# K and v steps chunk by chunk over three banks, with matmuls that keep the stationary operand

## The chip, the cores and the metric

One core of one Trainium2 chip. The metric is the device time of one execution in microseconds; the median of three runs stands for the kernel. TensorE multiplies (its weight loads are listed as an engine of their own, PEld), VectorE (DVE), ScalarE (ACT) and GpSimd (POOL) do the elementwise work, SyncE (SP) issues nearly all DMAs.

## The reference

x has 2048 tokens of 640 features. Branch A is a linear attention with 32 heads of 20 features, branch B a gated feed-forward block with 1728 hidden features; a sigmoid gate for each token mixes them.

```python
qkv = x @ wqkv                               # q, k, v: 32 heads of 20
pq, pk = q @ w_phi[h], k @ w_phi[h]          # head by head
phi_q = concat(softmax(pq), softmax(-pq))    # 40 features for each head
phi_k = concat(softmax(pk), softmax(-pk))
kv, z = phi_k^T v, sum_s phi_k
a = ((phi_q kv) / (phi_q z + 1e-6)) @ wo
b = (silu(x @ w_gate) * (x @ w_up)) @ w_down
out = g * a + (1 - g) * b                    # g = sigmoid(sum(x * gate_w))
```

## The kernel before

**Work.** Tokens go in 16 tiles of 128 (t), four of which make a group of 512 (bt). w_phi is multiplied into the k and q weights on the chip first, so that one product of x with wkv gives pk, a few columns of pq, v and the argument of the gate. There are four kinds of work on TensorE:

- gate and up for 14 blocks of hidden features (k) of a group: five matmuls of 512 columns each, then tanh and a copy on ScalarE, one operation on VectorE and one on GpSimd, which leave a block of hT
- a **k step** for each token tile (`ktile`, `features` with which = 1): 1441 columns of wkv in three parts, of 460 (the end of pk, q columns and some v), 481 (most of v and the gate) and 500 columns (the start of pk), each the sum over five chunks c of 128 input features. The stationary operand is the tile of x, `xT[:, c, tok]`; the weights are streamed
- a **q step** for each tile (480 columns of wq), whose features are turned by a DMA transpose, multiplied by the summed kv (`num`), divided, turned again and multiplied by wo (`wo`, and `worest` for the last 128 output features of a group)
- the sums over hT (`down` for each tile, `rest` for the last 128 output features of a group, `edge` for the last 64 hidden features)

**A k step before.** `features` adds three tasks, first (460 columns), main (481) and m_ (500), the second and third ordered behind the one before. Each goes through all five chunks into one bank of PSUM. The parts of 500 and 460 columns lie in a pair of neighbouring banks ("pair", key ps), the 481 in a third bank (key v). All three banks are taken when the first task starts. `vtail` evacuates: lines 991 and 993 copy the v part of the 460 columns (they count as writing the bank, so the max on VectorE waits for them), then line 996 copies the 480 columns of v and line 998 takes the tanh of the gate's column, which releases the bank "v". VectorE takes max (line 1066) and min (1070) and subtracts (1074, 1078), which releases the pair; then follow exp on ScalarE, sum (1089) and reciprocal (1093) on VectorE, the norm on GpSimd (1099) and a DMA transpose that SP issues (line 1115).

**Order.** `_Plan` works out the order of everything beforehand: each task has an engine, a cost, what it depends on, buffers that it takes and releases, a priority and for some a time before which it isn't begun ("hold", `K_AT + K_EACH * t` for k steps, `Q_AT + Q_EACH * t` for q steps). At every moment each engine gets its most urgent task that is ready and for whose buffers there is room; the program is written out in that order, and semaphore waits are put where the data needs them. So each engine runs a fixed order. `SUMS` gives the order of a group's sums around its edge ("x"), `D_AFTER` after which block of the next group they come. There are 8 banks of PSUM for all of it.

**A list of matmuls.** `mms` takes a list of (output, stationary, moving, first, last), works out the waits once for the whole list and issues one `pe.matmul` for each entry; each is a weight load and a matmul. The last one signals the semaphore.

Of the kernel before, what the change touches and what calls it, by code (L numbers as in the profile page):

```python
# [6 lines left out]
P = 128  # L7
# [15 lines left out]
VC = VG * GH * DH  # L23
# [6 lines left out]
VLO = VX + D - VC - DH  # L30
KVW = VLO + VC + 2
KB = 500
KOFF = 512 - KB
# [218 lines left out]
class _Plan:  # L252
# [11 lines left out]
    def add(self, eng, cost, fn, deps=(), prio=5.0, lat=None, acq=(), rel=(), name=""):  # L264
        t = _Task(eng, cost, fn, deps, prio, self.LAT[eng] if lat is None else lat,
                  tuple(acq), tuple(rel), len(self.tasks), name)
        self.tasks.append(t)
        return t
# [84 lines left out]
def _mm(*cols):  # L353
    return sum(c / 2400.0 + 0.003 for c in cols)


def _build(
# [13 lines left out]
    pe, act, dve, pool, sp = nc.tensor, nc.scalar, nc.vector, nc.gpsimd, nc.sync  # L371
# [8 lines left out]
    def sb(name, shape, dtype):  # L380
        t = nc.alloc_sbuf_tensor(name, list(shape), dtype)
        tr.reg_tensor(t, "sbuf", nc.lookup_mloc(t).addr, rowelems(shape), mybir.dt.size(dtype))
        return t
# [6 lines left out]
    xT = sb("xT", [P, 5, S_TOK], BF16)  # L390
    wq = sb("wq", [P, 5, QW], BF16)
    wkv = sb("wkv", [P, 5, KVW], BF16)
# [40 lines left out]
    ps = nc.alloc_psum_tensor("ps", [P, 8 * 512], F32)  # L433
# [6 lines left out]
    add = plan.add  # L440

    def bank(i, j, c0, c1, r0=0, r1=P):
        return ps[r0:r1, (2 * i + j) * 512 + c0:(2 * i + j) * 512 + c1]

    def one(b, c0, c1, r0=0, r1=P):
        return ps[r0:r1, b * 512 + c0:b * 512 + c1]

    def wide(i, n=D):
        return ps[:, 2 * i * 512:2 * i * 512 + n]

    def mms(groups):

        reads = [g[1] for g in groups] + [g[2] for g in groups]
        writes = []
        seen = set()
        for g in groups:
            k = (g[0].offset, str(g[0].ap))
            if k not in seen:
                seen.add(k)
                writes.append(g[0])  # L460

        def fn():
            last = None
            for o, l, r, st, sp_ in groups:
                last = pe.matmul(o, lhsT=l, rhs=r, start=st, stop=sp_, skip_group_check=True)  # L465
            return last
        return run("pe", fn, reads=reads, writes=writes)

# [82 lines left out]
    gw_l = add("act", 0.5, load_gate, prio=-7, lat=6.0, name="gw")  # L551
# [11 lines left out]
    def load_head(key, c0, c1, k0, k1, land, prio):  # L563
        w, src = (wg, gsrc) if key == "g" else (wu, usrc)
        t = load("sp", w[:, c0:c1, k0 * P:k1 * P], src[:, c0:c1, k0 * P:k1 * P], land, prio)
        for k in range(k0, k1):
# [17 lines left out]
    wv_l = [vx_l, load("sp", wkv[:, :, VX:VLO], rows(A_wqkv[:, 2 * D + VC:3 * D - DH]), 31.2, -35),  # L584
            load("sp", wkv[:, :, VLO:VLO + VC], rows(A_wqkv[:, 2 * D:2 * D + VC]), 32.0, -34.9)]
# [12 lines left out]
    xl = [x_[4] for x_ in xs]  # L598
# [153 lines left out]
        for k in range(HD):  # L752
            ffn_tail(0, k, cs[k], (last["g", k], last["u", k]), 0)

    K_AT, K_EACH, Q_AT, Q_EACH = 30.00, 6.722, 137.19, 6.955
    PRE_Q = 10.14
    PRE_EACH = 2.3
    PRE_AT = 23.6
    PRE_X = 27.0
    D_AFTER = 3  # L760
    FIN_DVE = 12
    SUMS = ((0, -1, "x", 1, 2, 3), (0, -1, "x", 1, 2, 3), (-1, 0, "x", 1, 2, 3), (0, -1, "x", 2, 1, 3))
    K_PAIRS = 9
    store_t = {}
    gs_t = {}
# [67 lines left out]
    def early(bt, j):  # L833
        return SUMS[bt].index(j) < SUMS[bt].index("x")

# [179 lines left out]
    def features(t, which, wq_l, prio, ctx):  # L1015

        tok = slice(t * P, (t + 1) * P)
        bt = t // 4  # L1020

        def cols(o_, w_, c0, c1):
            return lambda: mms(acc(o_(), [(xT[:, c, tok], w_[:, c, c0:c1]) for c in range(5)]))
        w_ = wkv if which else wq
        got = [("pair" if which else "bank", ctx, "ps"), ("phi", ctx, "phi"), ("st", ctx, "st"), ("pp", ctx, "pp")]
        ng = NKQ if which else NQ
        nh = GH * ng

        def cost(k, q):
            return k if which else q  # L1030
        if which:
            before = [kvp_t.get((bt - 2, h)) for h in range(2)]
            first = add("pe", _mm(*([VLO - KB] * 5)), cols(lambda: bank(ctx["ps"], 1, 0, VLO - KB), w_, KB, VLO),
                        deps=[xl[bt], gw_l] + wv_l + wq_l + before, prio=prio, acq=got + [("bank", ctx, "v")], name="p1")
            main = add("pe", _mm(*([VC + 1] * 5)), cols(lambda: one(ctx["v"], 0, VC + 1), w_, VLO, VLO + VC + 1), prio=0.0, name="v")
            main.after = first
            m_ = add("pe", _mm(*([KB] * 5)), cols(lambda: bank(ctx["ps"], 0, KOFF, 512), w_, 0, KB), prio=0.0, name="p1")
            m_.after = main
            vt = vtail(t, ctx, (first, main))
            start = first  # L1040
        else:
            start = m_ = add("pe", _mm(*([QW] * 5)), cols(lambda: one(ctx["ps"], 0, QW), w_, 0, QW), deps=[xl[bt]] + wq_l, prio=prio, acq=got, name="p0")
            vt = None
        start.hold = K_AT + K_EACH * t if which else Q_AT + Q_EACH * t

        def dst():
            return phi[:, ctx["phi"], 0:ng, 0:GF]

        def src():
            return wide(ctx["ps"], KOFF + nh * DH)[:, KOFF:KOFF + nh * DH] if which else one(ctx["ps"], 0, QW)  # L1050

        def pv():
            return src().rearrange("p (h f) -> p h f", f=DH)

        def pg():
            return src().rearrange("p (g k f) -> p g k f", k=GH, f=DH)

        def sv(sg):
            return dst().rearrange("p g (k s f) -> p g k s f", s=2, f=DH)[:, :, :, sg, :]

        def bc(tile):
            return tile[:, ctx["st"], 0:nh].rearrange("p (g k) -> p g k", k=GH).unsqueeze(3).to_broadcast([P, ng, GH, DH])

        def f_mx():
            a, b = mx[:, ctx["st"], 0:nh], pv()
            dveop(lambda: dve.tensor_reduce(a, b, AX.X, ALU.max), [b], [a])  # L1066

        def f_mn():
            a, b = mn[:, ctx["st"], 0:nh], pv()
            dveop(lambda: dve.tensor_reduce(a, b, AX.X, ALU.min), [b], [a])  # L1070

        def f_sp():
            o_, a, b = sv(0), pg(), bc(mx)
            dveop(lambda: dve.tensor_tensor(o_, a, b, ALU.subtract), [a, mx[:, ctx["st"], 0:nh]], [o_])  # L1074

        def f_sn():
            o_, a, b = sv(1), bc(mn), pg()
            dveop(lambda: dve.tensor_tensor(o_, a, b, ALU.subtract), [b, mn[:, ctx["st"], 0:nh]], [o_])  # L1078
        age = 2.5 + 0.01 * (t + (0 if which else NT))
        a1 = add("dve", cost(0.935, 0.565), f_mx, deps=[m_, vt], prio=age, name="max")  # L1080
        a2 = add("dve", cost(0.935, 0.565), f_mn, deps=[m_], prio=age, name="min")
        a3 = add("dve", cost(0.935, 0.565), f_sp, deps=[a1, a2], prio=age, name="sub")
        a4 = add("dve", cost(0.935, 0.565), f_sn, deps=[a2, a3], prio=age, rel=[got[0], ("pp", ctx, "pp")], name="sub")
        x1 = add("act", cost(1.5, 0.92), lambda: actop(dst(), dst(), ACTF.Exp), deps=[a4], prio=2, name="exp")

        def f_sm():
            a = sm[:, ctx["st"], 0:2 * nh].rearrange("p (g k) -> p g k", k=2 * GH)
            b = dst().rearrange("p g (k f) -> p g k f", f=DH)
            dveop(lambda: dve.tensor_reduce(a, b, AX.X, ALU.add), [b], [a])  # L1089

        def f_rc():
            a, b = rc[:, ctx["st"], 0:2 * nh], sm[:, ctx["st"], 0:2 * nh]
            dveop(lambda: dve.reciprocal(a, b), [b], [a])  # L1093

        def f_nm():
            a = dst().rearrange("p g (k f) -> p g k f", f=DH)
            r = rc[:, ctx["st"], 0:2 * nh]
            b = r.rearrange("p (g k) -> p g k", k=2 * GH).unsqueeze(3).to_broadcast([P, ng, 2 * GH, DH])
            poolop(lambda: pool.tensor_tensor(a, a, b, ALU.mult), [a, r], [a])  # L1099
        b1 = add("dve", cost(1.825, 1.075), f_sm, deps=[x1], prio=age, name="sum")  # L1100
        b2 = add("dve", cost(0.57, 0.37), f_rc, deps=[b1], prio=age, name="rec")
        return add("pool", cost(3.03, 1.75), f_nm, deps=[b2], prio=1, rel=[("st", ctx, "st")], name="norm")
# [140 lines left out]
    pre_k = premult_k(wkT_l, 2.0, PRE_AT)  # L1243
    pre_x = premult_x(wxT_l, 2.1, PRE_X)
    pre_q = premult_q(wqT_l, PRE_Q, 0.02)
# [7 lines left out]
    def downs_of(bt):  # L1253
        return [("d", j, bt) for j in SUMS[bt]]
    seq = [("f", k, bt) for k in range(K_PAIRS) for bt in range(2) if bt or k >= HD]
    seq += [("f", k, 0) for k in range(K_PAIRS, NK)]
    for bt in range(1, NBT):
        for k in range(K_PAIRS if bt == 1 else 0, NK):
            seq.append(("f", k, bt))
            if k == K_PAIRS * (bt == 1) + D_AFTER:  # L1260
                seq += downs_of(bt - 1)
# [72 lines left out]
```

## Time and profile before

| | us |
|---|---|
| median of 3 runs (285.13 to 285.67) | 285.41 |
| the profiled execution | 285.48 |
| its span | 283.7 |
| TensorE matmul busy / weight load busy | 278.8 / 137.2 |
| VectorE busy | 225.9 |
| ScalarE busy | 152.5 |
| GpSimd busy | 166.4 |
| matmuls of a k step, 3 x 80 records | 18.1 + 18.9 + 19.5 |
| granted TensorE clock | 1.00 |

The span is from the first to the last thing that the profiler saw. The time of the execution has some 1.8 us more around it. "PE" is the matmul, "PEld" the weight load, which runs beside it. Matmuls overlap one another, so their listed durations are longer than the distance from one start to the next. Most work of TensorE goes through one line of the program, 465, so shapes and names of tiles tell the groups apart: `ps<-wkv,xT` is a k step, `ps<-xT,wg` and `ps<-xT,wu` are gate and up, `ps<-v,phi` the products of features and v, `ps<-wd,hT` and `ps<-hT,wd` the sums over hT.

### The profile page before, as it was taken

The numbers are of one execution on the slowest core, as the hardware profiler recorded it, in microseconds if no ns is written. First come the engines' busy times: TensorE is split into PE (matmuls) and PEld (weight loads), VectorE is DVE, ScalarE is ACT, GpSimd is POOL, SyncE is SP. The second block draws the span as 40 slices with busy tenths as digits, with TensorE's granted clock in tenths as the row PEclk, the third lists the DMA queues.
The fourth block names the chain that finished last, engine by engine and source line by source line (L and its number), as shares of the span: only waits on it lengthen the run. The fifth ranks groups of instructions, "written<-read, shape, count | busy, mean of one in ns | idle before, by whom it ended". The sixth has DMA issues, their size and how long they took to land.

```text
span 283.7 us, 4489 instructions
## 1 busy us (share of the span) xinstructions
PE 278.8 (98%) x1671; PEld 137.2 (48%) x1700; DVE 225.9 (80%) x332; ACT 152.5 (54%) x272; POOL 166.4 (59%) x140
## 2 busy tenths in 40 slices
PE   8999999999999999999999999999999999999996
PEld 3444544444654455444544454454444454554543
DVE  0323369999899998999979989999989999974223
ACT  2555746777867465565634654566624666453320
POOL 4199613686667546447575394696865975962100
PEclk9999999999999999999999999999999999999999
DMA  7999999943000011000001021433556347254312
GB/s 169 270 126 147 288 228 160 288 145 72 14 16 2 12 25 37 14 2 14 17 14 32 15 52 38 83 62 60 62 116 177 58 84 190 59 103 85 116 37 92
DMA packets 74511, 25.41 MB, mean 90 GB/s; under 512 B 62585, under 2 KB 74489, under 8 KB 74489
## 3 DMA queue, kind: packets, MB, share of 16 engines
q1 hardware_dynamic: 73177, 25.10, 41.0%
q8 instruction: 13, 0.21, 0.3%
q10 hardware_dynamic: 1312, 0.03, 0.3%
q14 instruction: 9, 0.07, 0.1%
HBM read 8.46 MB, written 2.62 MB: 39 GB/s over the span
## 4 chain that ended last, share of the span: by engine, by line
PE 98%; issue 1%; DVE 0%
PE ps L465 97%; PE ps L645 2%; DVE xsb L795 0%
## 5 line engine op out<-in xcount | busy, mean ns | idle before, releaser
L695 POOL TENSOR_TENSOR hT<-hT,us 128x512 bf16<-128x512 bf16 (+1 forms) x56 | 62.2, 1119 | 56.9 <-DVE hT L686 30.0
L1099 POOL TENSOR_TENSOR phi<-phi,rc 128x1680 bf16<-128x1680 bf16 (+1 forms) x32 | 77.5, 2423 | 28.8 <-DVE rc L1093 28.6
L465 PE MATMUL ps<-xT,wg 128*128 128x512 bf16 (+1 forms) x287 | 67.2, 366 | 0.8
L465 PE MATMUL ps<-xT,wu 128*128 128x512 bf16 x254 | 63.1, 379 | 0.3
L686 DVE SCALAR_TENSOR_TENSOR hT<-hT,ps 128x512 bf16<-128x512 bf16 (+1 forms) x60 | 38.4, 644 | 29.5 <-ACT hT L475 26.9
L475 ACT ACTIVATE hT<-ps 128x512 bf16<-128x512 f32 (+1 forms) x60 | 33.8, 566 | 37.8 <-PE ps L465 37.5
L475 ACT ACTIVATE phi<-phi 128x1680 bf16<-128x1680 bf16 (+1 forms) x32 | 41.6, 1300 | 18.6 <-DVE phi L1078 18.5
L465 PE MATMUL ps<-wkv,xT 128*128 128x460 bf16 (+2 forms) x240 | 51.0, 366 | 0.1
L1089 DVE TENSOR_REDUCE sm<-phi 128x84 f32<-128x1680 bf16 (+1 forms) x32 | 48.3, 1512 | 3.0 <-ACT phi L475 3.0
L465 PE MATMUL ps<-wd,hT 128*128 128x512 bf16 (+4 forms) x230 | 48.6, 366 | 0.4
L465 PEld LDWEIGHTS ps<-xT,wg 128*128 128x128 bf16 x300 | 28.2, 98 | 29.3 <-issue 1.6
L690 ACT ACTIVATE us<-ps 128x512 bf16<-128x512 f32 (+1 forms) x60 | 33.7, 567 | 13.6 <-PE ps L465 12.3
L465 PEld LDWEIGHTS ps<-xT,wu 128*128 128x128 bf16 x260 | 25.4, 98 | 30.7 <-ACT xb L475 0.4
L465 PEld LDWEIGHTS ps<-wkv,xT 128*128 128x128 bf16 x240 | 23.2, 98 | 24.7
L465 PEld LDWEIGHTS ps<-wd,hT 128*128 128x128 bf16 (+1 forms) x238 | 21.7, 98 | 22.7 <-issue 0.2
L1066 DVE TENSOR_REDUCE mx<-ps 128x42 f32<-128x840 f32 (+1 forms) x32 | 26.4, 826 | 6.2 <-PE ps L465 6.2
L1070 DVE TENSOR_REDUCE mn<-ps 128x42 f32<-128x840 f32 (+1 forms) x32 | 26.6, 832 | 0.0
L1078 DVE TENSOR_TENSOR phi<-mn,ps 128x840 bf16<-128x840 f32 (+1 forms) x32 | 26.3, 821 | 0.3
L1074 DVE TENSOR_TENSOR phi<-ps,mx 128x840 bf16<-128x840 f32 (+1 forms) x32 | 26.4, 825 | 0.0
L807 POOL TENSOR_TENSOR xsb<-xsb,xb 128x512 bf16<-128x512 bf16 x12 | 13.8, 1151 | 13.4 <-ACT xb L475 13.4
L465 PE MATMUL ps<-wo,oT 128*128 128x512 bf16 x79 | 19.7, 379 | 0.1
L465 PE MATMUL ps<-wq,xT 128*128 128x480 bf16 x80 | 18.7, 366 | 0.0
(60 smaller groups left out, 206.6 us busy)
## 6 DMA issues: line engine op xcount, KB each, us to landing
out_dram<-xsb SPq DMA_DIRECT2D x15, 160.0 KB, 2.0
wd<-in_B_w_down_dram SPq DMA_DIRECT2D x1, 2080.0 KB, 9.7
wg<-in_B_w_gate_dram SPq DMA_DIRECT2D x2, 400.0 KB, 5.6
wu<-in_B_w_up_dram SPq DMA_DIRECT2D x2, 400.0 KB, 5.8
wo<-in_A_wo_dram SPq DMA_DIRECT2D x1, 800.0 KB, 5.5
wg<-in_B_w_gate_dram SPq DMA_DIRECT2D x2, 320.0 KB, 4.3
wu<-in_B_w_up_dram SPq DMA_DIRECT2D x2, 320.0 KB, 4.9
wkv<-in_A_wqkv_dram SPq DMA_DIRECT2D x1, 600.0 KB, 6.1
```

Of the source, the lines that this page charges most:

```text
L465: last = pe.matmul(o, lhsT=l, rhs=r, start=st, stop=sp_, skip_group_check=True)
L475: run("act", lambda: act.activation(o, i, func, scale=scale), reads=reads, writes=[o])
L686: dveop(lambda: dve.scalar_tensor_tensor(out=h, in0=h, scalar=1.0, in1=g_, op0=ALU.add, op1=ALU.mult), [h, g_], [h])
L690: run("act", lambda: act.activation(o_, u_, ACTF.Copy, scale=0.5), reads=[u_], writes=[o_] if k < 13 else [o_, u_])
L695: poolop(lambda: pool.tensor_tensor(h, h, u_, ALU.mult), [h, u_], [h])
L807: poolop(lambda: pool.tensor_tensor(x_, x_, b_, ALU.add), [x_, b_], [x_])
L1066: dveop(lambda: dve.tensor_reduce(a, b, AX.X, ALU.max), [b], [a])
L1070: dveop(lambda: dve.tensor_reduce(a, b, AX.X, ALU.min), [b], [a])
L1074: dveop(lambda: dve.tensor_tensor(o_, a, b, ALU.subtract), [a, mx[:, ctx["st"], 0:nh]], [o_])
L1078: dveop(lambda: dve.tensor_tensor(o_, a, b, ALU.subtract), [b, mn[:, ctx["st"], 0:nh]], [o_])
L1089: dveop(lambda: dve.tensor_reduce(a, b, AX.X, ALU.add), [b], [a])
L1099: poolop(lambda: pool.tensor_tensor(a, a, b, ALU.mult), [a, r], [a])
```

## The change

`mms` remembers the stationary operand of the entry before. Where an entry of the same list has the same one, it is issued by `again`, a matmul instruction that is marked to come without a weight load. Only the k steps have such entries one after another: their three tasks become one, and its list goes chunk by chunk, in each chunk the 460, the 481 and the 500 columns, so that the second and third matmul of a chunk find their operand in place. One task means one signal at the end: the copies of v, which waited for the first or the second task, now wait for the whole step. The plan's cost of the step is the sum of the three. Further, the due times of k and q steps, the earliest time of one weight product (PRE_X), D_AFTER and SUMS are other numbers.

```diff
+    def again(o, l, r, st, sp_):
+        return pe.add_instruction(mybir.InstMatmult(
+            name=nc.get_next_instruction_name(), engine=pe.engine, ins=[pe.lower_ap(r), pe.lower_ap(l)], outs=[pe.lower_ap(o)],
+            start_tensor_calc=st, stop_tensor_calc=sp_, tile_size=(P, P), tile_position=(0, 0), bass_skip_group_check=True, ldweights=False))
...
             last = None
+            held = None
             for o, l, r, st, sp_ in groups:
-                last = pe.matmul(o, lhsT=l, rhs=r, start=st, stop=sp_, skip_group_check=True)
+                key = (l.tensor.name, l.offset, str(l.ap))
+                if key == held:
+                    last = again(o, l, r, st, sp_)
+                else:
+                    last = pe.matmul(o, lhsT=l, rhs=r, start=st, stop=sp_, skip_group_check=True)
+                held = key
...
-    K_AT, K_EACH, Q_AT, Q_EACH = 30.00, 6.722, 137.19, 6.955
+    K_AT, K_EACH, Q_AT, Q_EACH = 31.00, 6.784, 138.78, 7.063
...
-    PRE_X = 27.0
-    D_AFTER = 3
+    PRE_X = 27.5
+    D_AFTER = 4
...
-    SUMS = ((0, -1, "x", 1, 2, 3), (0, -1, "x", 1, 2, 3), (-1, 0, "x", 1, 2, 3), (0, -1, "x", 2, 1, 3))
+    SUMS = ((0, -1, 1, "x", 2, 3), (-1, "x", 0, 1, 2, 3), (0, -1, 1, "x", 2, 3), (-1, 0, "x", 1, 2, 3))
...
-            first = add("pe", _mm(*([VLO - KB] * 5)), cols(lambda: bank(ctx["ps"], 1, 0, VLO - KB), w_, KB, VLO),
-                        deps=[xl[bt], gw_l] + wv_l + wq_l + before, prio=prio, acq=got + [("bank", ctx, "v")], name="p1")
-            main = add("pe", _mm(*([VC + 1] * 5)), cols(lambda: one(ctx["v"], 0, VC + 1), w_, VLO, VLO + VC + 1), prio=0.0, name="v")
-            main.after = first
-            m_ = add("pe", _mm(*([KB] * 5)), cols(lambda: bank(ctx["ps"], 0, KOFF, 512), w_, 0, KB), prio=0.0, name="p1")
-            m_.after = main
+
+            def all_of():
+                l = []
+                for c in range(5):
+                    for o_, c0, c1 in ((bank(ctx["ps"], 1, 0, VLO - KB), KB, VLO), (one(ctx["v"], 0, VC + 1), VLO, VLO + VC + 1),
+                                       (bank(ctx["ps"], 0, KOFF, 512), 0, KB)):
+                        l.append((o_, xT[:, c, tok], wkv[:, c, c0:c1], c == 0, c == 4))
+                mms(l)
+            first = main = m_ = add("pe", _mm(*([VLO - KB] * 5), *([VC + 1] * 5), *([KB] * 5)), all_of,
+                                    deps=[xl[bt], gw_l] + wv_l + wq_l + before, prio=prio, acq=got + [("bank", ctx, "v")], name="p1")
```

## The prediction

> **What bounds the kernel now.** The page first: its busy times, then its chain of work that ended last.
>
> ```profile
> span 283.7 us, 4489 instructions
> ...
> PE 278.8 (98%) x1671; PEld 137.2 (48%) x1700; DVE 225.9 (80%) x332; ACT 152.5 (54%) x272; POOL 166.4 (59%) x140
> ...
> PE 98%; issue 1%; DVE 0%
> PE ps L465 97%; PE ps L645 2%; DVE xsb L795 0%
> ```
>
> TensorE's matmuls are the chain from start to end. There are 1700 weight loads but 1671 matmuls: 29 matmul records are missing, and most "issue" pieces of 0.05 us in the chain are holes where one is missing. In the matmuls' order of time real idle time shows at three places: about 0.06 us before 64.00, 0.13 before 171.56 and 0.05 before 266.94, 0.24 us in all. So nothing but less time per matmul, or a shorter start or tail, can make this kernel faster by more than that, and any new wait of TensorE is paid in full.
>
> Next the timeline of TensorE alone (start, time to the end of the last, shape, count): is the load on the path?
>
> ```profile
> 120.60 3.21 PE L465 MATMUL ps<-wkv,xT 128*128 128x460 bf16 x15
> 123.64 1.24 PE L465 MATMUL ps<-xT,wg 128*128 128x512 bf16 x5
> 124.72 1.24 PE L465 MATMUL ps<-xT,wu 128*128 128x512 bf16 x5
> ...
> 135.32 0.86 PE L465 MATMUL ps<-v,phi 128*128 128x64 bf16 x24
> 136.01 1.34 PE L465 MATMUL ps<-wkv,xT 128*128 128x460 bf16 x6
> ```
>
> Read the starts, not the durations, since matmuls overlap. Five matmuls of 512 columns take 124.72 - 123.64 = 1.08 us, 216 ns each. Twenty-four of 64 columns take 136.01 - 135.32 = 0.69 us, 29 ns each. The line through both: (216 - 29) / 448 = 0.417 ns a column and 2.3 ns that don't depend on columns. A k step has 5 x (460 + 481 + 500) = 7205 columns in 15 matmuls: 7205 x 0.417 + 15 x 2.3 = 3.04 us, and the trace has 123.64 - 120.60 = 3.04. Now the loads by shape (busy us, mean ns, idle):
>
> ```profile
> L465 PEld LDWEIGHTS ps<-wkv,xT 128*128 128x128 bf16 x240 | 23.2, 98 | 24.7
> ...
> L465 PEld LDWEIGHTS ps<-v,phi 128*128 128x128 bf16 x176 | 6.2, 98 | 1.6 <-DVE kvacc L1149 0.2
> ```
>
> Both kinds are on record with 98 ns a load, yet the 64-column matmuls, each with a load of its own, follow one another at 29 ns. So a load costs at most 29 ns of TensorE's pace, and a k matmul gives it 194 to 211 ns of cover.
>
> **The change, part by part.** *160 loads fewer* (16 steps x 5 chunks x 2; 1700 become 1540). Their cover is the matmul before them, which stays. Upper bound of the gain: all of the 2.3 ns that don't depend on columns, 160 x 2.3 = 0.37 us. Lower bound: no row shows a matmul without a load. If it held back the next chunk's load until the third matmul has ended, each of 80 chunks would wait for up to one load of 98 ns, a loss of 7.8 us. I take 0: the rows show loads running ahead even at a pace of 29 ns, and the per-matmul remainder is as small at 64 columns as at 512, which reads like a cost of the matmul itself.
>
> The Trainium skill, "TensorE: Matmul & The Clock Gate", section "Back-to-back issue gap", says that a stream of pairs of load and matmul is paced by both, some 81 ns at 128 columns against 56 ns for a matmul alone. By that, an estimate, each of 160 loads taken away frees 25 ns, 4.0 us in all, and the sum would be 281.5. This trace disagrees: pairs with 64 columns go at 29 ns.
>
> *Chunk order over three banks.* The same 15 matmuls, the same columns: 0 on TensorE. The opening group of gate and up already goes round banks in this way, at the same 216 ns. What moves is the end: three groups that ended one after another end together. Here is a step and what follows it now (time, duration, in brackets the idle time before it).
>
> ```profile
> 136.01 3.21 PE L465 MATMUL ps<-wkv,xT 128*128 128x460 bf16 x15
> 137.19 0.32 ACT L991 ACTIVATE v<-ps 128x180 bf16<-128x180 f32 x1 [0.77 <-PE ps L465]
> 137.54 0.19 ACT L993 ACTIVATE v<-ps 128x20 bf16<-128x20 f32 x1
> ...
> 138.20 0.57 ACT L475 ACTIVATE v<-ps 128x480 bf16<-128x480 f32 x1 [0.47 <-PE ps L465]
> ...
> 138.81 0.17 ACT L998 ACTIVATE gtan<-ps 128x1 f32<-128x1 f32 x1
> ...
> 139.06 0.75 PE L465 MATMUL ps<-v,phi 128*128 128x64 bf16 x20
> ...
> 140.70 1.02 DVE L1066 TENSOR_REDUCE mx<-ps 128x42 f32<-128x840 f32 x1
> ```
>
> ScalarE starts on v 0.21 us after the first five matmuls now; it will start 0.21 us after all fifteen, at 139.27, 2.1 us later. The two copies (0.55 us with their gaps) then end at 139.82, the wide copy at 140.4 and the tanh, which frees v's bank, at 140.6 instead of 138.98: 1.6 us later in each of 16 steps. The max on VectorE conflicts with the two copies (same bank) and can start at 139.8 to 139.9 instead of 139.27, 0.6 us later. In this step VectorE comes at 140.70 anyway, so nothing is lost. How often it waits, and how often TensorE waits for a bank (total us, times, longest):
>
> ```profile
> DVE mx L1066 <- PE ps L465: 6.2, 4, 2.8
> ...
> PEld ps L465 <- ACT us L690: 0.7, 2, 0.4
> ...
> PEld ps L465 <- ACT gtan L998: 0.3, 1, 0.3
> ```
>
> The max waits directly for matmuls 4 times of 32, so the loss on VectorE is about 4 x 0.6 = 2.4 us, bounds 0 and 16 x 0.6 = 9.6. What is late next is subtraction, exponential, sum, the norm on GpSimd and the transposes that SP issues behind it. The busy times by stage (length, PE, PEld, DVE) say what hides it.
>
> ```profile
> 35.00:78.00 43.00, 42.78 (x239) 21.12 (x241) 38.80 (x44) 29.51 (x61) 23.34 (x14) 1.00 0.65 151
> ...
> 200.00:245.00 45.00, 44.68 (x275) 21.67 (x280) 42.92 (x77) 23.28 (x36) 32.69 (x25) 1.00 0.52 106
> 245.00:272.00 27.00, 26.79 (x170) 13.25 (x171) 13.43 (x29) 10.83 (x19) 10.54 (x9) 1.00 0.40 90
> ```
>
> Over the k and q steps VectorE is nearly full (95% from 200 to 245), but from 245 on it is half idle, 13.6 us of 27. And TensorE doesn't wait for it: gate, up and down matmuls stand between the steps and need no feature. Cost 0 while the plan has such work and a free bank at each point; without that cover it is the 1.6 us of one late bank, each time.
>
> *Due times and order.* The k steps are due 1.0 us later at first and 1.9 at last (31.00 + 15 x 6.784 = 132.76 against 130.83), the q steps 1.6 to 3.2 (244.73 against 241.52). The last q step now starts at 242.57, about 1 us after its due time. Its chain: num at 260.51, the product written at 262.62, the transpose issued by SP at 262.63 and landed a median 2.6 us later, 265.2; its wo matmuls start at 269.75. That leaves 4.5 us, more than 3.2, so the tail is not moved. Behind wo come 39 down matmuls and the worest, about 10 us, as before. D_AFTER 4 and the new SUMS change the order of sums that read finished hT tiles: the same matmuls, 0, and SP's queue gets the same transposes and stores, in stages where the DMA engines are busy 8 to 65% of the time. A new order could save the 0.24 us of idle time, or add as much again: I take +0.1.
>
> **The sum**, against the profiled run's own 285.48 us (span 283.7 and 1.8 around it; the median shown is 285.41, 0.07 less): loads 0, chunk order 0, order +0.1, together 285.6; on the footing of the median **285.5**. Of its own the case spans 285.0 to 286.0, with the runs shown spread over 0.54 us.
>
> **Rivals.** (1) *The 2.3 ns belong to the exchange of weights*, and matmuls that keep them save it: -0.37, 285.1. For it: every matmul of the trace has both, so the rows can't part them. Against: the line above needs no such term. 16%. (2) *Slower: the late bank.* TensorE's next group needs the bank that the tanh of line 998 frees. It happens already: at 63.76 a load waits 0.3 us for it and TensorE loses 0.06 us. Moved by 1.6 us, such a wait is no longer covered; it decides when no other of the eight banks is free as a k step ends. Once costs 1.6, 287.0; twice 288.6. For it: a step holds three banks at once, and the list above shows TensorE's loads waiting for evacuations. Against: the order is planned with the evacuations' costs, and gate and up need one bank each. 25%. (3) *The next chunk's load waits for the third matmul*: a quarter of its 7.8 us to all of them, 287.5 to 293.3. 4%. (4) *The loads are on the path after all*: by the rows at most 29 ns each, 160 x 29 = 4.6, 280.9; the 29 ns pace with loads speaks against it. 1%. The pace by the Trainium skill named above is this case. (5) *It doesn't do what it says*, a load is still put before each matmul: then 1700 loads are seen, and the time is that of my forecast, in which I count it. Forecast 54%.
>
> **How the numbers follow.** A difference under 0.2% (0.57 us, 284.84 to 285.98) can't be told from no change here. Faster: 1% of (4), a third of (1), a little of the forecast where the idle time goes too: 0.13. Slower: (2), (3) and 0.06 of the forecast: 0.35. The same: 0.52. The range reaches from 284.7 (rival 1 with the idle time saved) to 287.2 (one late bank); above it stand (3) and two late banks, about 12%, below it 3%. The likeliest case's own range is 285.0 to 286.0.
>
> **What would show it.** Loads: 1540, or 240 - 160 = 80 of wkv. The starts in a k step: 3.04 us from its first matmul to the next group means rival 1 is wrong, 3.01 that it is right (ten matmuls less by 2.3 ns each), over 3.2 rival 3. The idle time of TensorE between matmuls: 0.24 us as now, or waits over 1 us right behind a k step, put down to ScalarE's gtan or v copies (rival 2). The first copy of v should start 0.2 us behind the fifteenth matmul, the max some 0.6 us later than that. I am wrong if the start to 5.6 us or the tail behind the last matmul (281.3 to 283.7) changes, or if the last q step's sums end last.

## The result and the profile after

The changed kernel takes 287.50 us (median of 6 runs, 287.29 to 288.13) beside 285.34 us before (6 runs of the same job, 285.13 to 285.93): a ratio of 1.0077, interval 1.0062 to 1.0091. It is slower by 2.2 us, beyond the upper end of the range. The profiled execution took 288.13 us with a span of 286.4.

The page of the changed kernel: instructions by engine, and the chain that ended last.

```profile
span 286.4 us, 4353 instructions
...
PE 282.0 (98%) x1700; PEld 121.9 (43%) x1540; DVE 229.0 (80%) x332; ACT 150.3 (52%) x272; POOL 166.5 (58%) x140
...
PE 76%; DVE 20%; ACT 2%; issue 1%; DVEq 0%
```

The 160 loads are gone (1540) and the load busy time fell by 15 us, with no gain in time. What is new stands in the chain: 20% of it runs over VectorE, where before it was 0%. Put together from the starts of the matmuls, TensorE's idle time behind the first 11 us (what the edge has in both kernels left out) is 2.36 us at ten places, 0.24 before. VectorE's side of it, in the waits of the changed kernel (total us, times, longest):

```profile
DVE mn L1085 <- ACT v L1004: 4.4, 2, 3.5
...
DVE mn L1085 <- PE ps L475: 0.7, 1, 0.7
...
DVE mx L1081 <- PE ps L475: 0.5, 2, 0.3
```

Before, only the max waited, and for matmuls. Now the min waits, and for a copy of v. Where this starts can be seen at the first k step. First the kernel before, in the timeline:

```profile
35.35 5.82 PE L465 MATMUL ps<-wkv,xT 128*128 128x460 bf16 x28
...
36.52 0.32 ACT L991 ACTIVATE v<-ps 128x180 bf16<-128x180 f32 x1 [0.37 <-PE ps L465]
...
36.88 0.19 ACT L993 ACTIVATE v<-ps 128x20 bf16<-128x20 f32 x1
...
38.60 1.03 DVE L1066 TENSOR_REDUCE mx<-ps 128x42 f32<-128x840 f32 x1 [2.80 <-PE ps L465]
...
39.55 1.02 DVE L1070 TENSOR_REDUCE mn<-ps 128x42 f32<-128x840 f32 x1
```

And the changed kernel (lines 991, 993, 1066 and 1070 are 1002, 1004, 1081 and 1085 there):

```profile
39.06 0.32 ACT L1002 ACTIVATE v<-ps 128x180 bf16<-128x180 f32 x1 [2.45 <-PE ps L452]
...
39.41 0.19 ACT L1004 ACTIVATE v<-ps 128x20 bf16<-128x20 f32 x1
...
39.71 1.03 DVE L1085 TENSOR_REDUCE mn<-ps 128x42 f32<-128x840 f32 x1 [3.46 <-ACT v L1004]
...
40.66 1.02 DVE L1081 TENSOR_REDUCE mx<-ps 128x42 f32<-128x840 f32 x1
```

Before, the copies had ended at 37.07, and the max came 0.2 us behind the step, which ended at 38.40. Now they begin 0.2 us behind the step (which ends at 38.86), and VectorE begins only after them, 0.85 us behind the step. And VectorE's order has changed: min ahead of max.

The kernel's own plan says why. Its list of planned starts (`_build.log`) puts this min at 38.60 and the copies at 38.60 too, side by side. The copies are marked as writing the bank, so on the chip whichever comes second in the program waits. But `features` tells the plan of this for the max alone: a1 has `deps=[m_, vt]`, a2 (the min) has `deps=[m_]`, where vt is the copies. While the copies came during the step, the missing dependency was harmless, since the min never came before they were done. In the changed kernel the plan finds a free VectorE at the end of a step and a min that seems ready: it puts min ahead of max in 8 of 16 tiles, in 7 of them ahead of the planned end of the copies; the plan of before does so in none. The Trainium skill, "PSUM — Partial Sum Buffer", section "PSUM bank collisions raise a hardware error", gives a reason for such a mark: two engines must not access one bank at once. No run here shows that, and a kernel without the mark was not tried.

How the lag becomes idle time of TensorE shows in the changed kernel's chain (start, length, what). Two long stretches of VectorE in it begin with a min that waited, and each goes on, nearly all of it over VectorE, to an operation of line 697 and from there to TensorE:

```profile
39.71 1.03 DVE mn L1085
40.74 0.95 DVE mx L1081
...
49.05 0.61 DVE hT L697
49.79 4.67 PE ps L475 x21
...
73.75 1.03 DVE mn L1085
...
79.49 0.42 DVE hT L697
...
89.09 0.59 DVE hT L697
89.82 4.90 PE ps L475 x30
```

Four of the ten waits, 1.4 of the 2.36 us, lie in these two stretches. A third, from 149.96 to 160.54, begins with the late copies of v and a max behind the sixteenth step (0.4 us), a fourth, from 175.64 to 204.67, with a max of a q step (0.3 us). So for the later waits the chain alone doesn't show the min as the cause; the experiments have to.

Line 697 reads the product of gate and frees its bank. Here is one of the ten waits in the timeline:

```profile
159.72 0.68 DVE L697 SCALAR_TENSOR_TENSOR hT<-hT,ps 128x512 bf16<-128x512 bf16 x1
...
160.54 1.24 PE L475 MATMUL ps<-xT,wg 128*128 128x512 bf16 x5 [0.21 <-DVE hT L697]
```

VectorE ends at 160.40 and TensorE goes on 0.15 us later. It is the same at all ten places: an operation of VectorE that frees a bank ends 0.15 us before TensorE's next matmul. At eight it is line 697, at the other two lines 1093 (it frees the pair of a k step) and 1216 (it frees the pair of `num`). None of the ten follows a copy of v or the tanh that frees the bank of v. The longest, 0.65 us ahead of the seventh k step, has to be read with care:

```profile
80.03 0.10 PEld L475 LDWEIGHTS ps<-wkv,xT 128*128 128x128 bf16 x1 [0.58 <-issue]
80.06 0.35 PE L475 MATMUL ps<-wkv,xT 128*128 128x460 bf16 x1 [0.49 <-ACT us L701]
```

The list puts it down to a copy on ScalarE, but that copy ends at 80.06, when the matmul starts and its load is already running. What ended 0.15 us before is the operation of VectorE at 79.49 in the chain above, at 79.91.

VectorE's busy time rose by 3.1 us as well (225.9 to 229.0). Of this 2.3 us belong to two operations from 255.6 to 258.7 (line 825, 1.95 and 1.23 us long where such ones elsewhere take some 0.34). That is behind the last of TensorE's ten waits, at 204.67, so it is no part of the loss.

### The profile page after: what moved, and what is told of

It is laid out like the page before. It is cut to its first block, busy times and chain, and to the rows that moved or that the text cites. A ratio compares the mean times of both kernels' runs of the same rounds, so it can differ in the third digit from the quotient of the medians.

```text
span 286.4 us, 4353 instructions
## 1 busy us (share of the span) xinstructions
PE 282.0 (98%) x1700; PEld 121.9 (43%) x1540; DVE 229.0 (80%) x332; ACT 150.3 (52%) x272; POOL 166.5 (58%) x140
## 4 chain that ended last, share of the span: by engine, by line
PE 76%; DVE 20%; ACT 2%; issue 1%; DVEq 0%
PE ps L475 65%; PE ps L452 9%; DVE sm L1104 4%; DVE hT L697 4%; DVE phi L1089 3%; DVE mn L1085 2%; DVE mx L1081 2%; DVE phi L1093 2%; PE ps L656 2%; DVE ob L1216 1%; DVE rc L1108 1%; ACT phi L486 1%; DVE rd L1208 0%; DVE kvacc L1162 0%; ACT us L701 0%
## 5 line engine op out<-in xcount | busy, mean ns | idle before, releaser
L475 PE MATMUL ps<-xT,wg 128*128 128x512 bf16 (+1 forms) x300 | 70.1, 368 | 0.3 <-DVE hT L697 0.2
L475 PE MATMUL ps<-xT,wu 128*128 128x512 bf16 x260 | 64.3, 379 | 0.1
L475 PE MATMUL ps<-wd,hT 128*128 128x512 bf16 (+3 forms) x238 | 49.8, 366 | 0.0
L452 PE MATMUL ps<-wkv,xT 128*128 128x481 bf16 (+1 forms) x160 | 46.2, 370 | 0.0
L475 PE MATMUL ps<-wkv,xT 128*128 128x460 bf16 x80 | 28.5, 357 | 0.5 <-ACT us L701 0.5
L475 PEld LDWEIGHTS ps<-wkv,xT 128*128 128x128 bf16 x80 | 7.7, 96 | 35.7 <-issue 33.7
L1002 ACT ACTIVATE v<-ps 128x180 bf16<-128x180 f32 x16 | 5.1, 318 | 30.5 <-PE ps L452 30.5
```

Source lines behind the costliest of these rows:

```text
L452: return pe.add_instruction(mybir.InstMatmult(name=nc.get_next_instruction_name(), engine=pe.engine, ins=[pe.lower_ap(r), pe.lower_ap(l)], ...
```

## The experiments

The theory is that the min's wait, which the plan doesn't know of, makes VectorE late, and VectorE TensorE. Its measure is the distance between the chip and the kernel's plan: the start of a k step's first matmul in the trace, less its start in the plan's list (us).

| kernel | step 1 | 6 | 9 | 16 | growth 1 to 16 | TensorE idle |
|---|---|---|---|---|---|---|
| before | +0.02 | +0.01 | -0.01 | -0.15 | -0.17 | 0.24 |
| changed | +0.47 | +1.15 | +1.98 | +1.87 | 1.40 | 2.36 |
| after_again | +0.10 | +0.78 | +1.61 | +1.51 | 1.41 | 2.39 |
| loads_again | +0.16 | +0.84 | +1.66 | +1.56 | 1.40 | 2.38 |
| bank_order | -0.17 | +0.50 | +1.33 | +1.20 | 1.36 | 2.48 |
| old_numbers | +0.56 | +0.54 | +1.03 | +1.28 | 0.72 | 2.83 |
| min_dep_old_numbers | -0.26 | -0.29 | -0.02 | -0.19 | 0.07 | 0.52 |
| min_dep_tuned | -0.26 | -0.28 | -0.03 | -0.20 | 0.06 | 0.72 |
| two_banks_valid | +0.34 | +0.28 | +0.21 | +0.07 | -0.27 | 0.23 |

Chip and plan of the kernel before stay within 0.2 us of one another over all k steps. The five rows of kernels that signal once and don't tell the plan of the min's wait fall behind by 0.7 to 1.4 us; the other four don't. What the column of step 1 holds is the start of the kernel, which differs from run to run (the changed kernel has +0.47 in one execution and, as `after_again`, +0.10 in another).

**The load.** `loads` puts an ordinary load before every matmul and leaves the order of all instructions as it is.

```diff
-                if key == held:
+                if False:
```

> The changed kernel with an ordinary load before every matmul again (1700 loads), the order of all instructions else unchanged. Theory (loads are hidden with or without the change): the time of the changed kernel, 287.5 within 0.4, a k step still 3.05 us. Rival 1 of the prediction (2.3 ns a matmul come with the load): 0.37 us slower, 287.9, a k step 3.08 us. Rival (matmuls without a load are what costs): some 2 us less, 285.4.

Measured: 288.06 us (287.58 to 288.34), ratio 1.0091 (1.0077 to 1.0105). That is 0.56 over the 287.50 of the changed kernel and outside the 0.4 expected, while its k steps last as long. So both ran again on one chip (`after_again` is the changed kernel):

> The changed kernel once more, as the measure for loads_again on the same chip. Theory: 287.5 within 0.4.

> The changed kernel with a load before every matmul, beside after_again. The first look had it at 288.06, 0.56 above the changed kernel of another job, though its k step takes 3.05 us in both traces. Theory (loads hidden, the difference is the length of the slow first matmuls, which changes from run to run): within 0.3 of after_again. Rival 1 of the prediction: 0.4 us slower than after_again. Rival (loads cost more than that): 0.5 us slower or more.

Measured: the changed kernel 287.77 us (1.0086, 1.0072 to 1.0100), with loads 287.71 us (1.0084, 1.0070 to 1.0098). Side by side there is no difference: the loads cost nothing that can be measured. Here are two k steps one after another in the matmuls of TensorE, first without the second and third load of each chunk (the first matmul, the last two, and what follows):

```profile
113.35 0.36 PE L475 MATMUL ps<-wkv,xT 128*128 128x460 bf16 x1
...
119.04 0.58 PE L452 MATMUL ps<-wkv,xT 128*128 128x481 bf16 x2
119.45 0.81 PE L475 MATMUL ps<-wd,hT 128*128 128x512 bf16 x3
```

The same two with all loads:

```profile
113.41 6.26 PE L475 MATMUL ps<-wkv,xT 128*128 128x460 bf16 x30
119.51 0.81 PE L475 MATMUL ps<-wd,hT 128*128 128x512 bf16 x3
```

119.45 - 113.35 and 119.51 - 113.41 are both 6.10 us. Over all 16 steps the distance from first to fifteenth matmul is 2838.1 ns without and 2838.2 ns with the loads. Rival 1 of the prediction falls: the part of a matmul that doesn't depend on columns stays when its load goes.

**The one late signal.** `bank_order` keeps the single task and its plan, but the list goes through the chunks bank by bank, and each matmul loads (`(...)` stands for the list of the three banks).

```diff
-                for c in range(5):
-                    for o_, c0, c1 in (...):
+                for o_, c0, c1 in (...):
+                    for c in range(5):
```

> One task and one signal as in the changed kernel, but its list goes bank by bank as before, so every matmul loads again; same plan as the changed kernel. Theory (the one late signal matters, not the order of the matmuls): as the changed kernel, 287.5 within 0.5, and the min on VectorE waits for the copies of v behind the step. Rival (turning over three banks costs TensorE time): 285.4.

Measured: 287.50 us (287.44 to 287.60), ratio 1.0074 (1.0060 to 1.0087), with the same waits of the min as the changed kernel:

```profile
DVE mn L1085 <- ACT v L1004: 4.4, 2, 3.5
...
DVE mn L1085 <- PE ps L475: 1.0, 2, 0.7
```

So neither the order of the matmuls nor the missing loads made the kernel slower: it is as slow with the old order of matmuls and all loads. What is left is the one signal at the end and the new numbers. The order has a small price of its own: from first to fifteenth matmul a step takes 2830 ns bank by bank (before: 2831) and 2838 chunk by chunk, 8 ns x 16 = 0.13 us.

**What the plan is told.** `min_dep_old_numbers` is the changed code with one dependency more and the due times and orders of before; `old_numbers` has the same numbers without the dependency.

```diff
-        a2 = add("dve", cost(0.935, 0.565), f_mn, deps=[m_], prio=age, name="min")
+        a2 = add("dve", cost(0.935, 0.565), f_mn, deps=[m_, vt], prio=age, name="min")
```

> The changed code with one more dependency told to the plan (min on VectorE waits for the copies of lines 1002 and 1004, which it does on the chip in any case, as both use the bank), and the numbers of before (K_AT, PRE_X, D_AFTER, SUMS). The copies still come behind the whole step and the bank of v is still freed late. Theory (the changed plan orders min ahead of a wait it doesn't know of, VectorE falls behind the plan, and TensorE waits for VectorE): the plan of this one ends 0.27 us later than that of before, so 285.6 to 286.0, TensorE idle under 0.8 us between matmuls, and the sixteenth k step within 0.5 us of where the plan has it. Rival (the late copies and the late bank cost by themselves, rival 2 of the prediction): 286.9 or more, idle of 1.5 us or more.

> The changed code with the numbers of before, and nothing told to the plan. Theory: the plan itself has 1.6 us more idle TensorE time with these numbers, and VectorE falls behind it where min goes ahead of max, so 287 to 288.5. Rival (the new numbers alone made it slower): 285.4.

Measured: 285.68 us (11 runs, 285.44 to 286.04), ratio 1.0008 (0.9999 to 1.0017) with the dependency, 288.41 us, ratio 1.0106 (1.0092 to 1.0120) without. One word in a list of dependencies is worth 2.7 us here. The plans of the two account for half of it (their ends are 283.26 and 284.58, 1.3 us apart). Of the other 1.4 us, some 1.0 is idle time of TensorE that the plan without the dependency doesn't have (2.83 - 0.52 in the table, less the 1.3). The last 0.4 us isn't traced; in the two profiled executions the start alone differs by 0.8. Without the dependency the plan puts min ahead of max in 9 of 16 tiles, with it in none. With it, chip and plan agree at all 16 steps within 0.32 us, though the copies come as late and the bank of v is freed as late as in the changed kernel. The waits of the max and min:

```profile
DVE mx L1081 <- ACT v L1004: 3.5, 1, 3.5
...
DVE mx L1081 <- PE ps L475: 0.7, 2, 0.4
```

The one long wait is that of the first k step, when VectorE has nothing else to do; now it is the max that waits, as planned, and no min does. That the new numbers alone were to blame falls with `old_numbers`.

**The same with a plan as good as before.** `min_dep_tuned` has the dependency, and due times and SUMS chosen so that its plan ends where that of before ends.

```diff
-    K_AT, K_EACH, Q_AT, Q_EACH = 31.00, 6.784, 138.78, 7.063
+    K_AT, K_EACH, Q_AT, Q_EACH = 29.96, 6.722, 136.21, 7.201
...
-    PRE_X = 27.5
-    D_AFTER = 4
+    PRE_X = 27.0
+    D_AFTER = 3
...
-    SUMS = ((0, -1, 1, "x", 2, 3), (-1, "x", 0, 1, 2, 3), (0, -1, 1, "x", 2, 3), (-1, 0, "x", 1, 2, 3))
+    SUMS = ((0, -1, "x", 1, 2, 3), (0, -1, 3, 1, 2, "x"), (-1, 0, "x", 1, 2, 3), (0, -1, "x", 2, 1, 3))
```

> Chunk order, no second and third load, one late signal, the min's wait told to the plan, and due times with which the plan ends where that of before ends (282.98). Theory: as before, 285.4 within 0.4, TensorE idle under 0.7 us, the sixteenth k step within 0.4 us of its place in the plan. A gain over before of 0.3 or more would speak for rival 1 (160 x 2.3 ns); 286.5 or more for the late bank.

Measured: 285.93 us (11 runs, 285.62 to 286.57), ratio 1.0019 (1.0010 to 1.0028): 0.5 us over before, more than the 0.4 expected. The k steps are where the plan has them. Three waits of 0.29, 0.29 and 0.14 us, each for an operation of VectorE, make 0.72 us of idle time, 0.5 more than before (under 0.7 was expected), and the chunk order adds 0.13. Whether those waits come of the late copies or of this plan's other differences was not tried, so a price of the late copies up to 0.5 us stays open.

**Early copies.** `two_banks_valid` gives the 460 columns a task and signal of their own again and takes the other two banks chunk by chunk, the second matmul without a load; the min is not told of the copies.

```diff
+            first = add("pe", _mm(*([VLO - KB] * 5)), cols(lambda: bank(ctx["ps"], 1, 0, VLO - KB), w_, KB, VLO),
+                        deps=[xl[bt], gw_l] + wv_l + wq_l + before, prio=prio, acq=got + [("bank", ctx, "v")], name="p1")
...
+                    for o_, c0, c1 in ((one(ctx["v"], 0, VC + 1), VLO, VLO + VC + 1), (bank(ctx["ps"], 0, KOFF, 512), 0, KB)):
...
+            main = m_ = add("pe", _mm(*([VC + 1] * 5), *([KB] * 5)), two, prio=0.0, name="v")
+            main.after = first
```

> The 460 columns in a task and with a signal of their own as before, then the 481 and 500 chunk by chunk, the second without a load (80 loads fewer); min not told of the copies; due times with which the plan ends at 282.98. The copies that share a bank with min and max are early again, the wide copy of v and the release of its bank stay 1 us late. Theory (the unplanned wait of min is what cost): 285.4 to 285.9, no lag behind the plan. Rival (the late bank of v cost): 286.5 or more.

> As two_banks_tuned (the 460 columns first with a signal of their own, then 481 and 500 chunk by chunk, 80 loads fewer, min not told of the copies), with an order of sums in which the rest of every group comes ahead of its edge; the plan ends at 282.98 as that of before. Theory: no lag behind the plan at the k steps, TensorE idle under 0.5 us, 285.2 to 285.7, so within 0.3 of before. Rival (the late release of v's bank costs by itself): 286.5 or more.

Measured: 285.20 us (ratio 0.9992, 0.9983 to 1.0001) and 285.59 us (1.0005, 0.9996 to 1.0014); neither can be told from before, and the first is 0.2 us below what was expected. In the first of them one group's rest starts behind its edge and the edge opens its bank twice, so, by the code, part of the sum for 128 output features is left out there; the number of matmuls is the same. In the second the waits are those of the kernel before (6.2 us in 4 waits of the max there):

```profile
DVE mx L1083 <- PE ps L452: 6.1, 4, 2.8
...
DVE mx L1083 <- PE ps L475: 0.3, 1, 0.3
```

In both plans no min stands ahead of a max. Once the copies that share a bank with min and max come early, the missing dependency does no harm, and the later release of v's bank (some 1 us) costs nothing that can be measured. No version here was faster than before: the loads were hidden, and taking them away won nothing.

## Why the prediction was wrong

- **The loads: right.** 0 was taken between -0.37 and +7.8 us; the pair with and without loads shows 0 (287.71 and 287.77 us, steps equal to 0.1 ns). Rivals 1, 3 and 4 fall with it, and rival 5 with the 1540 loads. So does, for this kernel, the pace by pairs of load and matmul that the Trainium skill states in "TensorE: Matmul & The Clock Gate", section "Back-to-back issue gap": the estimate of 4.0 us from it is not seen.
- **The chunk order on TensorE: right but for 0.13 us** with three banks; with two (2831.0 ns a step) it costs none. Why three cost more is not shown.
- **What moves at the end of the step: seen, and priced at nothing. This step failed.** The prediction had the copies 2.1 us later and the max 0.6 us later (39.71 - 38.86 shows 0.85 behind the step's end, against 0.21 before: 0.6), named sum, norm and transposes as late next, worked out a loss of about 2.4 us on VectorE, and then set "Cost 0 while the plan has such work and a free bank at each point", because TensorE doesn't wait for features. The runs show 2.1 us more idle time of TensorE in its place. Two things were missed. VectorE does two jobs, and its order is fixed: when the min waits, the operations behind it that free banks come late too, and TensorE does wait for those, eight times of ten for the bank of gate. And the plan didn't know of the wait, so the cover it had laid out wasn't there. The line that says so, a2 with `deps=[m_]` just under a1 with `deps=[m_, vt]`, stood in the code. That 2.4 and 2.1 are near each other is chance: the 2.4 counts four waits of the max for matmuls, and the waits that cost are others.
- **Rival 2: the right side and the wrong mechanism.** It had the late release of v's bank as the price, and took as evidence against itself that "the order is planned with the evacuations' costs". Two kernels keep that late release and lose at most 0.5 us, and in the changed kernel the one load that waits for the tanh (0.5 us, at 85.94) costs TensorE nothing. Nor was the row on which this rival leans read at the right place: the wait of 0.3 us for the tanh is that of a load at 41.41, behind which TensorE loses nothing; at 63.76 the list shows 0.35 us of idle time without a releaser (the tanh had ended 0.12 us before, so the 0.06 us lost there may be its doing). The order was planned, and with one dependency too few. Its 287.0 was near the measured 287.5 by accident.
- **Due times and tail: right.** In the changed kernel the last matmul starts at 283.70 and the span ends 2.7 us later, as before (281.06 and 283.7). (Behind the last `wo` stand 52 `down` matmuls, not 39, since the last tile is summed in two parts; nothing in the sum hangs on it.)
- **The sum, put right:** idle time +2.1 (2.36 - 0.24), chunk order +0.13, loads 0: 2.25 us, against 2.16 and 2.33 measured beside before on two occasions. The profiled executions are 2.65 us apart, mostly because the changed one also began its first k step 0.46 us later. VectorE was 90 to 95% busy in the stages of the k and q steps, and the lag stays (+1.98 at step 9, +1.87 at step 16): what is lost there isn't won back by the last k step. How little room VectorE had was to be read from the lines shown.

## What to carry to other kernels

Here a load that the trace showed hidden was worth nothing when it was removed. Whether one is hidden can be read beforehand: compare the distance of starts at the smallest matmuls that have loads with the one at hand. What cost time was the signal that the regrouping moved. So list everything that waits for it, and where a program's order is worked out beforehand, check that the planner knows each of these waits: one that used to be fulfilled in time can be missing from it unnoticed. The start of each planned step in the trace, less its start in the plan, shows between which steps the time is lost. And the releaser that a list names is to be compared with the times: one that ends as the wait is over can't have ended it.

## What the runs showed that was not expected

- Fifteen matmuls that go round three banks take 8 ns longer than bank by bank (2838 and 2830 ns from first to fifteenth start), with or without the loads. What makes the difference is open. The opening group, which goes round four, had shown 216 ns a matmul as elsewhere.
- The start differs from run to run. In the changed kernel's first profile the first 14 distances between matmuls are 381 to 427 ns, in that of before the first 12 are 377 to 427, and in some runs a matmul of the opening group waits up to 0.9 us for a load of x. The first k step of the kernels in the table, planned at 35.34 in all of them, starts between 35.1 and 35.9 us. The times of before differ by about as much (285.13 to 285.93 in six runs); how much of that is the start wasn't traced.
